# Running the next unit's scores directly behind each unit's values in a fused attention and expert kernel

## The chip, the cores and the metric

The kernel runs on one core of a Trainium2 chip. The metric is the device time of one execution in microseconds (us). Five engines work side by side: PE (TensorE, the matrix array, with its weight loads listed as PEld), DVE (VectorE), ACT (ScalarE), POOL (GpSimd) and SP (SyncE, which issues most transfers). Each runs its own instructions in the order in which the program lists them and waits on semaphores of the others.

## What is computed

Three layers, one behind the other, all in fp32 accuracy:

```python
# 1: attention with a decaying state, B=4 sequences, H=8 heads, 768 steps, D=48
f = 1 / (1 + exp(-f_logit))
for t in range(768):
    state = f[t][:, None] * state + outer(k[t], v[t])
    y[t] = q[t] @ state
# 2: x is y as 3072 rows of 384
h = x @ w_in                      # 384 x 2048
x = (h - tanh(h)) @ w_out         # 2048 x 384
# 3: each row with x @ w_skip > 0 goes to the expert of its largest x @ w_gate
out = x + gate * (relu(x @ w1[e]) @ w2[e])     # 8 experts, 384 x 1024 x 384
```

## The kernel before

**Attention.** The 768 steps of a sequence are cut into 6 chunks of 128; a chunk of one sequence, with all 8 heads, is a unit `u`, and there are 24 of them (`u = 4 * chunk + sequence`). Two units make a block `blk` of 256 rows for layer 2. The steps of a unit, all written in `attend(u)`, are:

- preparation: `lhi`, `llo` (DVE, split the logarithms of f), `pl` (PE, running sums over the chunk, L421), `ek`, `en` (ACT), `mk`, `mq` (DVE, L433 and L436), `tk`, `tq` (PE, transposes, L446) and `ck`, `cq` (ACT, copies out of PSUM);
- `scores` (PE): 32 matmuls q·k (L467) on 48 rows by 64 columns of the array, and from the second chunk on 16 matmuls of q with the old state S (L476), which start the unit's output `py`;
- two `mask` steps (DVE, L496);
- `values` (PE): 16 matmuls of the masked scores with v, added to `py` (L508, 128 rows by 48 columns), and behind them 16 for the change of the state, `pu` (L515, 128 rows by 64 columns);
- `out1`, `out2` (ACT, L537, L538, L541) copy `py` out of PSUM, `renew` (DVE, L559) adds `pu` to S, and `decay` (POOL) multiplies S.

**Layer 2.** Each block has 16 slots. Slot `n` holds `G` (9 matmuls into `ph`, L651) and `H` of the slot two before (6 matmuls into `po`, L691); between them lie `T` and `ghi` on ACT, `bend` on DVE (L663) and `glo` on POOL (L674). Behind a block's last slot its rows are routed (`dot`, L233 on DVE; `pp`, L718 and L719 on PE).

**PSUM.** The pools `pa`, `yp`, `ph` and `po` have two banks each. `scores` takes both banks of `pa` (given back by the masks) and both of `yp` (given back by `out1` and `out2`); `pu`, `pl`, `tk`, `tq` and `pp` take one bank of `pa` each. Block 1 of layer 2 uses `yp` for its sums, so unit 6 can take it only when that block is done.

**The order of the instructions.** For all of attention and the first 10 blocks of layer 2 a planner, `in_order`, sets the order before the program is built. Each step has an engine, a cost in us, the steps that it comes after, the banks that it takes and gives, and a key. The planner repeats: of all steps that can begin, take the one that could begin first, and of equal ones that with the smallest key. The keys are slot numbers; `at(pos)` gives those of attention, 32 slots ahead of the block that needs the unit, the second unit of a block 6 slots behind the first. `T`, `bend`, `ghi` and `glo` have keys 1000 lower than all others. What the planner leaves is one fixed list for each engine. The first 6 units (`FIRST`) run while w_in and w_out are loaded and decoded in 16 chunks (`abs`, `shift`, `stt1`, `stt2`, `hi`, `lo`, mostly on DVE), with keys from -65 up in steps of 6. The last 2 blocks and layer 3 follow in an order written by hand.

Of the kernel before, what the change touches and what calls it, by code (L numbers as in the profile page):

```python
# [9 lines left out]
F32 = mybir.dt.float32  # L10
# [12 lines left out]
LO_BITS = 2.0**-15  # L23
HI_BITS = float.fromhex("0x1.dffffep+16")
MARK = 2.0**-96


class Step:


    def __init__(self, key, eng, cost, emit, after, take, give, moved, lag):
        self.key, self.eng, self.cost, self.emit = key, eng, cost, emit
        self.after, self.take, self.give, self.moved, self.lag = after, take, give, moved, lag
        self.done = None


def in_order(steps, bufs):


    waiting, heirs, ready = {}, {}, []  # L40
    for x in steps:
        waiting[x] = len(x.after)
        for a in x.after:
            heirs.setdefault(a, []).append(x)
        if not x.after:
            ready.append(x)
    taken = {p: [] for p in bufs}
    ended = {}
    free = {}
    left, since, out = {}, 0.0, []  # L50

    def begin(x):
        t = max((a.done + (a.lag if a.eng != x.eng else 0.0) for a in x.after), default=0.0)
        n = {}
        for p, _ in x.take:
            i = len(taken[p]) + n.get(p, 0) - bufs[p]
            n[p] = n.get(p, 0) + 1
            if i >= 0:
                if i >= len(taken[p]) or taken[p][i] not in ended:
                    return None  # L60
                t = max(t, ended[taken[p][i]])
        return max(t, free.get(x.eng, 0.0))

    while ready:
        t, _, _, x = min((t, x.key, i, x) for i, x in enumerate(ready) for t in (begin(x),) if t is not None)
        ready.remove(x)
        free[x.eng] = end = t + x.cost
        if x.moved:
            past = end - since
            while past > 0 and any(left.values()):  # L70
                busy = [e for e in left if left[e]]
                d = min(past / len(busy), min(left[e] for e in busy))
                for e in busy:
                    left[e] = left[e] - d if left[e] - d > 1e-6 else 0.0
                past -= d * len(busy)
            since = max(since, end)
            mine = left[x.eng] = left.get(x.eng, 0.0) + x.moved
            end = since + mine + sum(min(left[e], mine) for e in left if e != x.eng) + 2.0
        x.begun, x.done = t, end
        for p, a in x.take:  # L80
            taken[p].append((p, a))
        for g in x.give:
            ended[g] = end + x.lag
        out.append(x)
        for h in heirs.get(x, ()):
            waiting[h] -= 1
            if not waiting[h]:
                ready.append(h)
    assert len(out) == len(steps), "steps that can never begin"
    return out  # L90
# [3 lines left out]
def decay_attention_moe_kernel(  # L94
# [15 lines left out]
    P = 128  # L110
    B, H, T, D = q.shape
# [15 lines left out]

    AHEAD = 2
    FIRST, NJOIN, NPAY, SKEW = 6, 4, 6, 0
    EARLIEST, LEAD = -100, 32  # L130
    ALONE = 4
    CHUNK0, CHUNK, LATE = -65, 6, 4
    QUEUE = (0, 1, "w", 2, 3, "w", "w", "u", "u", "u", 4, 5, "w", "u")
# [240 lines left out]
        )  # L374
        yield

    xT, xfs, dds = {}, {}, {}

    def side(p, j):

# [4 lines left out]
    def step(name, key, eng, cost, emit, *after, take=(), give=(), moved=0.0, lag=0.15):  # L385

        made[name] = x = Step(key, eng, cost, emit, after, take, give, moved, lag)
        steps.append(x)

    def attend(u):  # L390
# [11 lines left out]
        m = {}  # L402

        def at(pos):
            return (NF * blk - LEAD if u > FIRST - 1 else EARLIEST + 12 * blk) + 6 * half + pos

        def lhi():
            m["hl"] = apool.tile([P, 2, H * D], F32R, tag="lfs", name=f"lfs{u}", bufs=1)
# [49 lines left out]
        def scores():  # L458
            kT, qT = m["kT"], m["qT"]
            ps = m["ps"] = [pa.tile([P, 512], F32, tag="pa", name=f"ps{u}_{j}") for j in range(2)]  # L460
            py = m["py"] = [yp.tile([P, 512], F32, tag="yp", name=f"py{u}_{j}") for j in range(2)]

            def score(p):
                for a in range(2):
                    for j in range(2):
                        r = slice(64 * j, 64 * j + D)
                        nc.tensor.matmul(  # L467
                            ps[j][64 * a : 64 * a + 64, p * P : (p + 1) * P], lhsT=kT[r, p, 64 * a : 64 * a + 64],
                            rhs=qT[r, p], start=True, stop=True,
                        )  # L470

            def recall(p):
                for j in range(2):
                    r = slice(64 * j, 64 * j + D)
                    o, w = 64 * side(p, j), (64, D)[side(p, j)]
                    nc.tensor.matmul(  # L476
                        py[j][o : o + w, p % 2 * P : p % 2 * P + P], lhsT=S[b][r, p, :w], rhs=qT[r, p],
                        start=(p % 2 == 0), stop=False,
                    )

            for p in range(2):
                score(p)
                if c:
                    recall(p)
                    recall(p + 2)
                else:
                    nc.tensor.matmul(
                        py[p][:64, : 2 * P], lhsT=S[b][:, 0].bitcast(BF16)[:, :64],
                        rhs=ones[:112, None, :].to_broadcast([112, 2, P]), start=True, stop=False,
                    )  # L490
                score(p + 2)
# [11 lines left out]
        def values():  # L503
            vt, py = loaded["v", u], m["py"]
            for p in range(NP):
                for j in range(2):
                    o = 64 * side(p, j)
                    nc.tensor.matmul(  # L508
                        py[j][o : o + D, p % 2 * P : p % 2 * P + P], lhsT=vt[:, 2 * p + j], rhs=m["A", j][:, p],
                        start=(c == 0 and o > 0 and p % 2 == 0), stop=(p % 2 == 1),  # L510
                    )
            pu = m["pu"] = pa.tile([P, 512], F32, tag="pa", name=f"pu{u}")
            for h in range(H):
                p, j = divmod(h, 2)
                nc.tensor.matmul(  # L515
                    pu[64 * j : 64 * j + 64, p * D : (p + 1) * D], lhsT=kp[:, h], rhs=vt[:, h], start=True, stop=True
                )
            if u < FIRST:
                for h in range(H):
                    p, j = divmod(h, 2)  # L520
                    nc.tensor.matmul(
                        pu[64 * j : 64 * j + 64, 2 * P + p : 2 * P + p + 1], lhsT=e8[:, h], rhs=ident[:, P - 1 :],
                        start=True, stop=True,
                    )
# [72 lines left out]
        if u >= FIRST:  # L597
# [3 lines left out]
        step(("tq", u), at(1.5), "PE", 0.44, turn4("q", qp4), ("mq", u), ("tk", u), take=((pk_in, f"q{u}"),), lag=0.25)  # L601
        step(("cq", u), at(1.5), "ACT", 0.59, copy4("q"), ("tq", u), ("scores", u - 2), give=((pk_in, f"q{u}"),))
        step(
            ("scores", u), at(2), "PE", 1.5 if c else 1.0, scores, ("ck", u), ("cq", u), ("decay", u - B), ("values", u - 1), 
            take=[("pa", f"s{u}{j}") for j in range(2)] + [("yp", f"y{u}{j}") for j in range(2)], lag=0.25,
        )
        for j in range(2):
            step(
                ("mask", u, j), at(2.5), "DVE", 0.68, mask(j), ("scores", u), ("values", u - 2),
                ("mask", u, j - 1) if j else None, give=(("pa", f"s{u}{j}"),),  # L610
            )
        step(("values", u), at(3), "PE", 1.7 if u < FIRST else 1.3, values, ("mask", u, 1), ("v", u), take=(("pa", f"u{u}"),), lag=0.25)
        step(
            ("out1", u), at(3.5), "ACT", 0.6, out1, ("values", u), ("xlo", u - 1 - half) if blk > 1 else None, ("out2", u - 1),
            give=(("yp", f"y{u}1"),),
        )
        step(("out2", u), at(3.5), "ACT", 0.38, out2, ("out1", u), give=(("yp", f"y{u}0"),))
        old = [("decay", 2 * blk - 4), ("decay", 2 * blk - 3), ("in_range", 2 * blk - 3)]
        step(
            ("renew", u), at(3.5), "DVE", 0.5 if u < FIRST else 0.36, renew, ("values", u),  # L620
            *(old if u < FIRST and half == 0 else []), give=(("pa", f"u{u}"),),
        )
        if u < FIRST:
# [116 lines left out]
        yield  # L740

    def route(u):
        pt = pay.pop(u)
        lg = rpool.tile([P, E + 1], F32, tag="lg", name=f"lg{u}")
        yield from dots(rpool, pt[:, :DM], f"{u}", wb, lg)
        yield from place(pt, lg, u)

    def route_now(u):

        pt = pay.pop(u)  # L750
        px = pa.tile([P, 512], F32, tag="pa", name=f"px{u}")[:, :DM].rearrange("p (k t) -> p k t", k=KT)
        for i in range(KT):
            nc.tensor.transpose(px[:, i], pt[:, i * P : (i + 1) * P], ident)
# [242 lines left out]

    for u in range(NU):
        blk, half = divmod(u, 2)
        e = EARLIEST + 6 * u if u < FIRST else NF * blk - LEAD + 6 * half - 8

        def get(nm, u=u):
            return lambda: load_in(nm, u)
# [29 lines left out]
    for n, (b, f) in enumerate(slots):  # L1032
# [12 lines left out]
        if n < len(slots) - LAG:  # L1045
# [6 lines left out]
            if f == NF - 1:  # L1052
                for u in (2 * b, 2 * b + 1):
                    step(
                        ("fin", u), n + LAG, "ACT", 0.5, (lambda u=u: finish1(u)), ("H", n), ("scat", u - NPAY),
                        ("wb", 0), ("fill", 0) if u == NPAY - 1 else None, give=((p, f"o{b}{u % 2}"),),
                    )
                    step(("out", u), n + LAG + 1, "SP", 0.45, (lambda u=u: finish2(u)), ("fin", u), moved=1.1)
# [431 lines left out]
```

## Time and profile before

| | |
|---|---|
| three timed runs | 734.79, 735.40, 737.32 us, median 735.4 us |
| the profiled execution | 737.04 us, of which the profile's span is 734.9 us |
| mean granted clock of TensorE | 0.988 of full speed |
| PE busy | 696.7 us, 95% of the span |
| DVE, ACT, POOL busy | 67%, 50%, 39% of the span |

The span runs from the first to the last instruction. A busy share is a mean over stages; starts of instructions are measured, ends of matmuls are modelled, so costs on PE are best read from one start to the next.

### The profile page before, as it was taken

Reading aid. Unit: us, or ns where it says so; the run is one execution under the profiler, and the core shown is the slowest. Engines: PE = TensorE matmul, PEld = TensorE weight load, DVE = VectorE, ACT = ScalarE, POOL = GpSimd, SP = SyncE. Lnnn points to the kernel's source line nnn. Section 1 sums busy time; section 2 is a strip of 40 time slices with the busy share of each in tenths; the row PEclk is TensorE's granted clock in tenths of the full one; section 3 lists DMA queues with packets and bytes.
Section 4 is the critical chain, followed back from the end, with each engine's and each line's share of the span. In section 5 each row is a group of like instructions: output and inputs, shape, how many; then the busy total and the mean of one; then the engine's idle time right before and its main releaser. Section 6 shows DMA issues by size and latency. Waiting matters only on the chain. (4 is left out here: it accounts for less than half of the span.)

```text
span 734.9 us, 16491 instructions
## 1 busy us (share of the span) xinstructions
PE 696.7 (95%) x6168; PEld 655.8 (89%) x6168; DVE 491.9 (67%) x1390; ACT 367.0 (50%) x882; POOL 283.2 (39%) x316
## 2 busy tenths in 40 slices
PE   5889989999999999999999999999989899999993
PEld 3678989999998999999999999999989689999993
DVE  2678999678777968768685775845583845655530
ACT  3576786446444465456545444444434435555530
POOL 1232443423344343442434343434543314555641
PEclk9999999999999999999999999999999999999997
DMA  9979793833321312222221220033002667666500
GB/s 155 234 136 220 160 158 80 310 64 72 76 39 40 80 37 70 44 61 44 63 61 28 60 42 32 2 97 115 13 28 71 205 202 236 213 207 211 175 14 22
DMA packets 152688, 76.77 MB, mean 104 GB/s; under 512 B 113864, under 2 KB 149337, under 8 KB 152470
## 3 DMA queue, kind: packets, MB, share of 16 engines
q1 hardware_dynamic: 149462, 70.48, 38.6%
q0 software_dynamic: 2848, 5.00, 1.9%
q8 instruction: 50, 0.82, 0.5%
q14 instruction: 40, 0.33, 0.2%
q10 hardware_dynamic: 288, 0.15, 0.1%
HBM read 61.60 MB, written 15.86 MB: 105 GB/s over the span
## 5 line engine op out<-in xcount | busy, mean ns | idle before, releaser
L674 POOL TENSOR_TENSOR gs<-th,gs 128x256 fp32r<-128x256 f32 x190 | 168.1, 889 | 249.5 <-ACT gs L668 225.0
L691 PE MATMUL po<-uhi,gs 128*128 128x384 f32 x768 | 230.6, 343 | 2.0 <-POOL gs L674 1.8
L651 PE MATMUL ph<-xT,whi 128*128 128x256 f32 x1152 | 219.9, 287 | 2.7 <-DVE th L663 1.8
L651 PEld LDWEIGHTS ph<-xT,whi 128*128 128x128 f32 x1152 | 183.9, 189 | 8.0 <-DVE th L663 3.6
L651 PE MATMUL ph<-xT,wlo 128*128 128x256 f32 x576 | 162.6, 282 | 0.0
L691 PEld LDWEIGHTS po<-uhi,gs 128*128 128x128 f32 x768 | 142.4, 190 | 6.4 <-POOL gs L674 3.8
L663 DVE TENSOR_TENSOR th<-ph,th 128x256 f32<-128x256 f32 x192 | 79.9, 419 | 90.8 <-ACT th L658 90.1
L233 DVE CUSTOM_DVE_ANT_0 scr<-pay,wb 128x384 f32<-128x384 f32 x198 | 128.0, 647 | 7.9 <-ACT pay L699 4.1
L691 PE MATMUL po<-ulo,gs 128*128 128x384 f32 x384 | 129.8, 338 | 0.4 <-DVE ulo L372 0.4
L658 ACT ACTIVATE th<-ph 128x256 f32<-128x256 f32 x192 | 72.7, 381 | 113.2 <-PE ph L651 75.9
L668 ACT ACTIVATE gs<-th 128x256 fp32r<-128x256 f32 x192 | 79.2, 416 | 96.4 <-DVE th L663 92.7
L651 PEld LDWEIGHTS ph<-xT,wlo 128*128 128x128 f32 x576 | 109.5, 190 | 0.0
L691 PEld LDWEIGHTS po<-ulo,gs 128*128 128x128 f32 x384 | 73.2, 191 | 0.7 <-DVE ulo L372 0.7
L1150 PE MATMUL eh<-xt,w 128*128 128x256 f32 x504 | 69.6, 283 | 0.0
L1174 PE MATMUL eo<-w,h 128*128 128x384 f32 x336 | 69.1, 342 | 0.0
L1150 PEld LDWEIGHTS eh<-xt,w 128*128 128x128 f32 x504 | 67.0, 188 | 0.4
L1174 PEld LDWEIGHTS eo<-w,h 128*128 128x128 f32 x336 | 56.3, 188 | 0.0
L1159 DVE SCALAR_TENSOR_TENSOR h<-eh,h 128x256 fp32r<-128x256 f32 x56 | 23.7, 423 | 45.5 <-ACT h L1158 45.5
L1158 ACT ACTIVATE h<-eh 128x256 fp32r<-128x256 f32 x56 | 21.5, 385 | 61.9 <-PE eh L1150 61.8
L732 POOL DMA_INDIRECT xs<-pay,di x24 | 25.7, 1069 | 65.5 <-DVE sm L245 31.2
L317 POOL TENSOR_TENSOR w<-r,w 128x768 fp32r<-128x768 f32 x24 | 44.1, 1846 | 12.3 <-ACT w L316 12.2
L891 POOL DMA_INDIRECT out_dram<-yo,xa x16 | 15.7, 979 | 69.3 <-DVE yo L899 33.6
(189 smaller groups left out, 927.8 us busy)
## 6 DMA issues: line engine op xcount, KB each, us to landing
r<-in_moe_w_dram SPq DMA_DIRECT2D x56, 384.0 KB, 5.1
stgu<-in_moe_w_out_dram SPq DMA_DIRECT2D x4, 1536.0 KB, 7.0
f<-in_f_logit_dram SPq DMA_DIRECT2D x24, 192.0 KB, 3.5
stgw<-in_moe_w_in_dram SPq DMA_DIRECT2D x24, 192.0 KB, 5.5
out_dram<-pay SPq DMA_DIRECT2D x24, 192.0 KB, 2.9
k<-in_k_dram SPq DMA_DIRECT2D x22, 192.0 KB, 3.3
q<-in_q_dram SPq DMA_DIRECT2D x22, 192.0 KB, 3.3
v<-in_v_dram SPq DMA_DIRECT2D x22, 192.0 KB, 2.8
```

The lines of the kernel that those rows point to most:

```text
L233: nc.vector.tensor_tensor_reduce(out=scr, in0=x, in1=wb[:, n], scale=1.0, scalar=0.0, op0=ALU.mult, op1=ALU.add, accum_out=lg[:, n : n + 1])
L317: eng.tensor_tensor(lo, raw, hi.bitcast(F32), ALU.subtract)
L651: nc.tensor.matmul(ph, lhsT=w[:, i, fs], rhs=x[:, i, a], start=(n == 0), stop=(n == 3 * KT - 1))
L658: nc.scalar.activation(th, ph, AF.Tanh)
L663: nc.vector.tensor_tensor(th, ph, th, ALU.subtract)
L668: nc.scalar.activation(t[:, 0], th, AF.Copy)
L674: eng.tensor_tensor(t[:, 1], th, t[:, 0].bitcast(F32), ALU.subtract)
L691: nc.tensor.matmul(po[blk, s], lhsT=t[:, a, ss], rhs=w[:, f], start=(f == 0 and n == 0), stop=(f == NF - 1 and n == 2))
L732: nc.gpsimd.indirect_dma_start(xs[:, :], bass.IndirectOffsetOnAxis(ap=di[:, :], axis=0), pt[:, :], None, bounds_check=E * NT - 1, oob_is_e ...
L1150: nc.tensor.matmul(ph, lhsT=a1[:, w, i, f * P : (f + 1) * P], rhs=xt[:, i, a], start=(n == 0), stop=(n == 3 * KT - 1))
L1159: nc.vector.scalar_tensor_tensor(out=h[:, 1], in0=ph, scalar=0.0, in1=h[:, 0].bitcast(F32), op0=ALU.max, op1=ALU.subtract)
L1174: nc.tensor.matmul(eo[e, s], lhsT=h[:, a, ss], rhs=a2[:, w, f], start=(f == 0 and n == 0), stop=(f == NF2 - 1 and n == 2))
```

## The change

For units from 6 on, `values` is cut in two: `pu` (the 16 matmuls for the state) comes first, at the key that `values` had, and the 16 matmuls into `py` follow as `values`. `renew` now waits for `pu` alone. `values`, and the `scores` of the unit after it, get the key -2000, and the planner counts them as if they could begin 0.5 us earlier (`NEXT`), so that PE goes on with `pu`, `values`, and the next unit's `scores`. So that this unit is ready by then, the steps of preparation get keys 12 lower (`PREP`), as do the loads and the logarithms that feed them, and all of attention 4 lower (`LEAD` 36 in place of 32). The two outputs `py` of successive units lie in the left and right halves of the same two banks of `yp`, which are taken once at unit 6 and not given back; `scores` of a unit comes after `out2` of the unit two before. In the planner each change of PE between these three kinds of step and all others costs 0.2 us (`CHANGE`). The rest keeps `pay` tiles in their table and has `fin` come after the write of the rows that used the same buffer.

```diff
+CHANGE, NEXT = 0.2, 0.5
...
     while ready:
-        t, _, _, x = min((t, x.key, i, x) for i, x in enumerate(ready) for t in (begin(x),) if t is not None)
+        t, _, _, x = min((t - x.ahead, x.key, i, x) for i, x in enumerate(ready) for t in (begin(x),) if t is not None)
+        t += x.ahead
         ready.remove(x)
+        if x.eng == "PE" and x.parts != parts:
+            t, parts = t + CHANGE, x.parts
...
-    EARLIEST, LEAD = -100, 32
+    EARLIEST, LEAD, PREP = -100, 36, 12
...
+        x.parts = name[0] in ("scores", "pu", "values")
+        x.ahead = NEXT if key == -2000 else 0.0
...
-            return (NF * blk - LEAD if u > FIRST - 1 else EARLIEST + 12 * blk) + 6 * half + pos
+            return (NF * blk - LEAD - (PREP if pos < 2 else 0) if u > FIRST - 1 else EARLIEST + 12 * blk) + 6 * half + pos
...
-            py = m["py"] = [yp.tile([P, 512], F32, tag="yp", name=f"py{u}_{j}") for j in range(2)]
+            if u <= FIRST:
+                halves[:] = [yp.tile([P, 512], F32, tag="yp", name=f"py{u}_{j}") for j in range(2)]
+            o = 2 * P * (u % 2) if u >= FIRST else 0
+            py = m["py"] = [t[:, o : o + 2 * P] for t in halves]
...
+            if u < FIRST:
+                update()
+
+        def update():
+            vt = loaded["v", u]
             pu = m["pu"] = pa.tile([P, 512], F32, tag="pa", name=f"pu{u}")
...
         step(
-            ("scores", u), at(2), "PE", 1.5 if c else 1.0, scores, ("ck", u), ("cq", u), ("decay", u - B), ("values", u - 1), 
-            take=[("pa", f"s{u}{j}") for j in range(2)] + [("yp", f"y{u}{j}") for j in range(2)], lag=0.25,
+            ("scores", u), -2000 if u > FIRST else at(2), "PE", 1.5 if c else 1.0, scores, ("ck", u), ("cq", u), ("decay", u - B), ("values", u - 1),
+            ("out2", u - 2), take=[("pa", f"s{u}{j}") for j in range(2)] + ([("yp", f"y{u}{j}") for j in range(2)] if u <= FIRST else []), lag=0.25,
         )
...
-        step(("values", u), at(3), "PE", 1.7 if u < FIRST else 1.3, values, ("mask", u, 1), ("v", u), take=(("pa", f"u{u}"),), lag=0.25)
+        if u >= FIRST:
+            step(("pu", u), at(3), "PE", 0.4, update, ("mask", u, 1), ("v", u), take=(("pa", f"u{u}"),), lag=0.25)
+            step(("values", u), -2000, "PE", 0.9, values, ("pu", u), lag=0.25)
+        else:
+            step(("values", u), at(3), "PE", 1.7, values, ("mask", u, 1), ("v", u), take=(("pa", f"u{u}"),), lag=0.25)
...
-        e = EARLIEST + 6 * u if u < FIRST else NF * blk - LEAD + 6 * half - 8
+        e = EARLIEST + 6 * u if u < FIRST else NF * blk - LEAD - PREP + 6 * half - 8
...
-                        ("fin", u), n + LAG, "ACT", 0.5, (lambda u=u: finish1(u)), ("H", n), ("scat", u - NPAY),
+                        ("fin", u), n + LAG, "ACT", 0.5, (lambda u=u: finish1(u)), ("H", n), ("scat", u - NPAY), ("out", u - NPAY),
```

## Rows read from the trace of the kernel before

**Rows 1.** The page's busy time, share of the span and instructions, for PE.

```profile
PE 696.7 (95%) x6168; PEld 655.8 (89%) x6168; DVE 491.9 (67%) x1390; ACT 367.0 (50%) x882; POOL 283.2 (39%) x316
```

**Rows 2.** Windows: length, then busy us and instructions by engine, clock, transfers.

```profile
100.00:120.00 20.00, 18.53 (x126) 17.29 (x125) 19.90 (x27) 14.61 (x33) 8.37 (x9) 1.00 0.76 150
...
140.00:490.00 350.00, 347.31 (x3495) 330.46 (x3495) 260.46 (x850) 175.64 (x460) 134.43 (x159) 1.00 0.24 55
```

**Rows 3.** Waits of PE from 140 to 500 us: total, times, longest.

```profile
PE po L691 <- POOL gs L674: 1.5, 2, 0.9
...
PE py L508 <- DVE A L496: 0.3, 2, 0.2
```

**Rows 4.** Timeline of PE around one unit's scores: start, duration, what.

```profile
328.13 0.34 PE L691 MATMUL po<-uhi,gs 128*128 128x384 f32 x1
328.40 0.45 PE L467 MATMUL ps<-qT,kT 48*64 48x128 f32 x8
328.67 0.40 PE L476 MATMUL py<-qT,S 48*64 48x128 f32 x8
328.89 0.62 PE L467 MATMUL ps<-qT,kT 48*64 48x128 f32 x16
329.32 0.40 PE L476 MATMUL py<-qT,S 48*64 48x128 f32 x8
...
329.87 0.44 PE L691 MATMUL po<-uhi,gs 128*128 128x384 f32 x1
```

**Rows 5.** Timeline of PE around the same unit's values.

```profile
332.19 1.08 PE L508 MATMUL py<-A,v 128*48 128x128 f32 x16
333.11 0.62 PE L515 MATMUL pu<-v,kp 128*64 128x48 f32 x16
333.66 0.44 PE L691 MATMUL po<-uhi,gs 128*128 128x384 f32 x1
333.94 0.34 PE L691 MATMUL po<-ulo,gs 128*128 128x384 f32 x1
334.11 0.51 PE L691 MATMUL po<-uhi,gs 128*128 128x384 f32 x2
```

**Rows 6.** Timeline of the weight loads behind those values.

```profile
333.00 0.60 PEld L515 LDWEIGHTS pu<-v,kp 128*64 128x64 f32 x16
333.65 0.19 PEld L691 LDWEIGHTS po<-uhi,gs 128*128 128x128 f32 x1
```

**Rows 7.** Weight loads of an early unit, from a half-wide tile to transposes.

```profile
31.02 0.55 PEld L521 LDWEIGHTS pu<-ident,en 128*64 128x64 f32 x16
31.59 0.41 PEld L446 LDWEIGHTS pk<-ident,early 128*112 128x112 f32 x4
```

**Rows 8.** Timelines of PE and DVE: `pu` and `renew`, the latest of 18 and a usual one.

```profile
305.50 0.62 PE L515 MATMUL pu<-v,kp 128*64 128x48 f32 x16
...
306.81 0.35 DVE L559 TENSOR_TENSOR S<-pu,S 112x192 f32<-112x192 f32 x1
...
333.77 0.36 DVE L559 TENSOR_TENSOR S<-pu,S 112x192 f32<-112x192 f32 x1
```

**Rows 9.** Timeline of ACT: `out1` (first copy) and `out2`.

```profile
333.56 0.26 ACT L537 ACTIVATE tm<-py 112x128 f32<-112x128 f32 x1
...
333.87 0.39 ACT L541 ACTIVATE xf<-py 112x256 f32<-112x256 f32 x1
```

**Rows 10.** Timeline of the loading stage, DVE and PE: preparation of units 6 and 7.

```profile
92.44 0.35 DVE L409 CAST lfs<-f 128x384 fp32r<-128x384 f32 x1
92.83 0.56 DVE L412 TENSOR_TENSOR lfs<-f,lfs 128x384 fp32r<-128x384 f32 x1
...
120.81 0.55 DVE L433 TENSOR_TENSOR kp<-k,kp 128x384 f32<-128x384 f32 x1
121.27 1.10 DVE L436 TENSOR_TENSOR qp<-q,en 128x384 f32<-128x384 f32 x1
...
92.85 0.44 PE L421 MATMUL pl<-lfs,tri 128*128 128x384 f32 x1 [1.72 <-DVE lfs L409]
```

More of the change, by code (lines that the diff above doesn't have):

```diff
@@ L34, in __init__ @@
         self.done = None
+        self.parts, self.ahead = False, 0.0
 def in_order(steps, bufs):
@@ L50, in in_order @@
     left, since, out = {}, 0.0, []
+    parts = False
     def begin(x):
@@ L375, in unpack @@
         yield
-    xT, xfs, dds = {}, {}, {}
+    xT, xfs, dds, halves = {}, {}, {}, []
     def side(p, j):
@@ L611, in attend @@
             )
-        step(("values", u), at(3), "PE", 1.7 if u < FIRST else 1.3, values, ("mask", u, 1), ("v", u), take=(("pa", f"u{u}"),), lag=0.25)
+        if u >= FIRST:
[3 more added lines that the diff above has]
+            step(("values", u), at(3), "PE", 1.7, values, ("mask", u, 1), ("v", u), take=(("pa", f"u{u}"),), lag=0.25)
         step(
             ("out1", u), at(3.5), "ACT", 0.6, out1, ("values", u), ("xlo", u - 1 - half) if blk > 1 else None, ("out2", u - 1),
-            give=(("yp", f"y{u}1"),),
+            give=(("yp", f"y{u}1"),) if u < FIRST else (),
         )
-        step(("out2", u), at(3.5), "ACT", 0.38, out2, ("out1", u), give=(("yp", f"y{u}0"),))
+        step(("out2", u), at(3.5), "ACT", 0.38, out2, ("out1", u), give=(("yp", f"y{u}0"),) if u < FIRST else ())
         old = [("decay", 2 * blk - 4), ("decay", 2 * blk - 3), ("in_range", 2 * blk - 3)]
         step(
-            ("renew", u), at(3.5), "DVE", 0.5 if u < FIRST else 0.36, renew, ("values", u),
+            ("renew", u), at(3.5), "DVE", 0.5 if u < FIRST else 0.36, renew, ("values" if u < FIRST else "pu", u),
             *(old if u < FIRST and half == 0 else []), give=(("pa", f"u{u}"),),
@@ L742, in route @@
     def route(u):
-        pt = pay.pop(u)
+        pt = pay[u]
         lg = rpool.tile([P, E + 1], F32, tag="lg", name=f"lg{u}")
@@ L748, in route_now @@
     def route_now(u):
-        pt = pay.pop(u)
+        pt = pay[u]
         px = pa.tile([P, 512], F32, tag="pa", name=f"px{u}")[:, :DM].rearrange("p (k t) -> p k t", k=KT)
```

## The prediction

> **What bounds the kernel now.** I read the page first, then windows, waits and the timeline of single units. PE is busy for 95% of the span, no other engine for more than 67% [rows 1]. In the stage where units 6 to 23 run, from 140 to 490 us, PE is busy 347.3 of 350 us at full granted clock while DVE has 90 us and ACT 174 us to spare [rows 2]. The idle 2.7 us there go mostly to late `gs` tiles, which the change does not touch, and 0.3 us to masks that `values` waited for [rows 3]. So time can be won in this stage only by giving PE less to do. The number of matmuls stays the same; what may shrink is what PE loses where small tiles of the array follow whole ones. The start, by contrast, is bound by DVE: from 100 to 120 us it is busy 19.90 of 20 us and PE idles 1.47 us [rows 2].
>
> **The change part by part, first the price of a switch.** Ends of matmuls are modelled, so I count from start to start. Within `H` one matmul follows another after 334.11 - 333.94 = 0.17 us [rows 5].
>
> Going into `scores`: the last matmul of `H` starts at 328.13, so the next could start at 328.30; it starts at 328.40, 0.10 us later. The first 8 take 0.27 us, where 16 in the middle take 0.43, so 0.215 for 8: 0.05 us more [rows 4]. Sum 0.15.
>
> Coming back from `pu`: its 16 weight loads begin at 333.00 and end at 333.60, the next load begins at 333.65: 0.05 us. Then the first matmul of `H` needs 333.94 - 333.66 = 0.28 us in place of 0.17, since its weights could not be loaded ahead: 0.11 us [rows 5, 6]. Sum 0.16.
>
> From `values` to `pu`, both on tiles of 128 rows by half the columns, 16 matmuls take 333.11 - 332.19 = 0.92 us [rows 5], that is 57 ns each for 128 columns, and I see no step at the joint. Turning the two round costs and saves nothing.
>
> **What the joint removes and adds.** For units 7 to 23, 17 times, one return (0.16) and one entry (0.15) vanish: 0.31 us. In their place stands one step from `values` (128 rows) to `scores` (tiles of 64 rows) that the trace does not show at full speed. It costs from nothing, as between `values` and `pu`, to 0.31 us, if the narrower row tiles need both the emptying and the late weights. The one half-wide tile followed directly by another form without PE waiting lost 31.59 - 31.57 = 0.02 us [rows 7], but that went to whole tiles. The nearest row is the entry into `scores` itself, from 128 rows to 64: 0.15 us. I take it. Gain 0.16 us a joint, 17 x 0.16 = 2.7 us, bounds 0 and 5.3.
>
> The planner's own count makes the step from `values` to `scores` free; that alone would give 5.3 us. A rule speaks against it. The Trainium skill (TensorEngine Tiling (Array Packing), Key Properties) says that a change of the tiling mode, not of the tile alone, drains the array, and it lists 128x64 and 64x64 as different modes; by it three of the four drains of a unit would stay. The rows agree so far: a gap into `scores` [rows 4], none within one mode [rows 5]. The sum by the rule is the one I took.
>
> **What the joint may wait for.** `scores` needs both banks of `pa`, one held by `pu` until `renew` has read it. From the start of `pu` to the end of `renew` passes 334.13 - 333.11 = 1.02 us as usual, and 307.16 - 305.50 = 1.66 us at worst [rows 5, 8]. With `pu` first and `values` behind it PE is busy for 0.55 + 0.92 = 1.47 us, and the step takes 0.15. So `values` hides `renew`; without this cover every joint would pay 0.4 us. The worst case leaves 0.05 to 0.2 us once: 0.1 us lost. The planner may let PE idle up to 0.5 us for `scores`; that is a rival below.
>
> **The halves of a bank.** If the reading of one half and the writing of the other are kept apart, `out1` of a unit, issued behind the next `scores`, waits until these are done, 1.5 us later. Queued behind it on ACT are `out2`, copies of the preparation, and later `T` and `ghi`. During the chain of 0.55 + 0.92 + 1.5 = 3 us PE finishes no `G`, so the `T` and `ghi` of the last one run before `out1`, and the next `T` is due only after it; ACT has half its time free [rows 2]. I cost it at nothing; without the cover it would be up to 1 us each time.
>
> **Masks, preparation, loads.** `pu` now comes well after its masks, not 2 to 4 us behind `scores`: the 0.3 us of waits [rows 3] go. Preparation 12 slots earlier changes no work; `pl` of a unit still waits for `values` of the unit two before, so in the steady stage it lies in PE's stream as now. The earlier loads (f, k, q, v on SP's queue) still wait for the same weight load and pass only later entries. In the start it is a rival. `CHANGE` makes the plan's 2.8 us for a pair of `scores` and `values` 3.2, near the real 1.47 + 1.47 + entries and returns: fewer small waits at best, which I do not price. The edits to `pay` and `fin` cost nothing: the write of a row block is long done when its buffer comes round.
>
> **The sum.** -2.7 - 0.3 + 0.1 = -2.9 us. The profiled run took 737.0 us with a span of 734.9; the same shape would give a span of 732.0 and a run of 734.1. That execution is at the top of the three runs; from their median of 735.4 the sum gives 732.5 us.
>
> **Rivals.**
> 1. *The joint is free* (one mode, as the planner counts). For: [rows 7]. Against: the entry into `scores` [rows 4]. 17 x 0.31 = 5.3, with the other terms -5.5: 729.9 us.
> 2. *The change doesn't show*: the step from `values` to `scores` costs as much as the two that it replaces, or the plan finds preparation or `renew` late and puts a `G` between, so that few joints exist. For: `renew`'s margin is thin in the plan (0.25 + 0.36 + 0.15 against 0.9 us), and DVE is 74% busy [rows 2]. Gain 0 to 1: about 735 us.
> 3. *The start gets slower.* Keys of preparation for units 6 and 7 fall from 16 and 22 to 0 and 6, ahead of the last chunks of the weights (keys 1 to 25), and the `CHANGE` cost shifts the plan of units 0 to 5. One unit's `lhi`, `llo`, `mk`, `mq` are 0.35 + 0.56 + 0.55 + 1.10 = 2.6 us on the engine that bounds this stage [rows 10]; two units 5.1 us, if PE waits for all of it. `pl` has already cost PE 1.72 us there. Against: `lhi` of unit 6 ran at 92.4 us, ahead of chunks with smaller keys, so time and not key decided. At the full price: 732.5 + 5.1 = 737.6 us. It decides once over 2.9 us are lost before 140 us. The other unit's preparation can't move there, since `pl` of unit 8 waits for `values` of unit 6.
> 4. *A bank as a lock on PE.* If the plan puts `out1` and `out2` ahead of the next `scores`, its 16 matmuls into the other half wait for the copies, which end 334.26 - 333.56 = 0.7 us after they begin [rows 9], some 1.0 us after `values`, less 0.2 us of q·k work first: 17 x 0.8 = 14 us, 746 us. Against: `scores` may go 0.5 us ahead and `out1` is planned 0.25 us behind `values`. The Trainium skill (PSUM — Partial Sum Buffer, PSUM bank collisions raise a hardware error) holds that TensorE and ScalarE must not touch one bank and quadrant at once, whatever the columns; no row here shows two units in one bank.
>
> **How the numbers follow.** Forecast 0.43, at 732.5 us, its own range 730.5 to 734 (waits and the step's cost by a third either way); rival 1 0.13; rival 2 0.20; rival 3 0.16; rival 4 0.04; 0.04 for a gain beyond rival 1 from a tighter plan. A measurement tells 0.3%, 2.2 us, from no change: faster is below 733.2, slower above 737.6. Two thirds of the forecast's 0.43 lie below 733.2 (0.29), and with rival 1 and the last case 0.46, to which rival 2's better plans add 0.04: faster 0.50. Rival 3 gives 0.10 slower and 0.06 same, rival 4 0.04 slower, and 0.02 of rival 2 falls there with a worse plan: slower 0.16. The rest is the same, 0.34. The range leaves out rival 4, half of rival 1 and of the gains beyond it, and the upper end of rival 3: 729.5 to 737.5.
>
> **What would show it.** In the timeline: `pu`, `values`, `scores` in one block for units 6 to 23, 17 joints. From the last matmul of `values` to the first of `scores` a gap near 0.10 us and no idle time released by `renew`. `out1` starting about 1.5 us later behind `values`. PE's idle time in the stage near 2.4 us. The length of the stretch from unit 6's scores to unit 23's values, for the same slots, 3 us shorter, and the start up to there unchanged within 1 us. Wrong if `renew` releases PE at joints, if `G` or `H` lie between `values` and the next `scores`, if the start moves by more than 2 us, or if `gs` tiles come later because ACT is held up.

## The result

| | before | after |
|---|---|---|
| median of four runs each | 736.36 us (734.79 to 738.49) | 746.30 us (744.79 to 749.23) |
| ratio after / before, 95% interval | | 1.0143 (1.0113 to 1.0173) |
| profiled execution, its span | 737.04, 734.9 us | 749.23, 747.3 us |
| mean granted clock | 0.988 | 0.979 |

The change costs 9.9 us. The forecast was 732.5 us with a range up to 737.5: wrong in sign, and outside.

From the page of the kernel after, busy time by engine and the clock in 40 slices:

```profile
PE 705.4 (94%) x6168; PEld 659.1 (88%) x6168; DVE 483.5 (65%) x1390; ACT 366.0 (49%) x882; POOL 286.5 (38%) x316
...
PEclk9978999999999999999999999999999999999997
```

The clock on the page of the kernel before:

```profile
PEclk9999999999999999999999999999999999999997
```

The same 6168 matmuls keep PE busy 8.7 us longer than in [rows 1], and the third and fourth slices, 37 to 75 us, show a lower clock than before. So the loss isn't only idle time, and a part of it lies where no joint is yet. (Line numbers differ between kernels: in the kernel after, `G` is L672, `H` L712, `scores` L479 and L488, `values` L520, `pu` L532 and `renew` L576.)

To place it I read three points in each timeline: the start of unit 6's scores (called S6), a matmul near the end of the planned part (P: 559.3 us before, 572.0 after) and the end. S6 is 141.45 us before and 150.27 after, with the same number of `G` and `H` ahead of it: **8.8 us lost in the start**. From S6 to P, 417.85 us became 421.7: **3.9 us lost in the steady stage**, where a gain was forecast. From P to the end 175.6 became 175.3. (The sum is that of two single executions, 12.2 us apart; the one after was the slowest of its four.)

**The start.** Windows of the kernel after, and the same of the kernel before behind it; columns as in [rows 2]:

```profile
40.00:60.00 20.00, 18.27 (x180) 15.49 (x177) 13.51 (x25) 13.49 (x32) 7.33 (x7) 0.74 0.71 116
60.00:80.00 20.00, 16.69 (x207) 15.02 (x206) 14.42 (x23) 11.99 (x29) 4.92 (x7) 0.83 0.79 185
```

```profile
40.00:60.00 20.00, 16.82 (x163) 13.29 (x167) 17.41 (x29) 16.18 (x38) 7.10 (x9) 0.94 0.77 155
60.00:80.00 20.00, 20.00 (x284) 19.14 (x277) 16.64 (x28) 11.49 (x28) 7.68 (x8) 0.97 0.84 177
```

From 40 to 60 us PE is busier after than before and DVE has 3.9 us less work: the matmuls are slow (clock 0.74), and what DVE needs from them seems to come late; that this is why DVE has less to do is read from the order, and no run tests it alone. From 60 to 80 us PE makes 207 matmuls instead of 284. The timeline of PE after, from this stretch:

```profile
42.35 0.49 PE L827 MATMUL pg<-ident,wg 128*9 128x128 f32 x3 [1.20 <-DMA wg<-in_moe_w_skip_dram]
...
49.34 0.63 PE L672 MATMUL ph<-xT,whi 128*128 128x256 f32 x2
49.77 0.41 PE L672 MATMUL ph<-xT,wlo 128*128 128x256 f32 x1
49.98 0.63 PE L672 MATMUL ph<-xT,whi 128*128 128x256 f32 x2
...
53.78 1.08 PE L520 MATMUL py<-A,early 128*48 128x128 f32 x16
...
66.86 0.38 PE L672 MATMUL ph<-xT,whi 128*128 128x256 f32 x1 [2.70 <-ACT xT L597]
```

And two lines of that of the kernel before, the values of the same unit 3 and S6:

```profile
45.37 1.08 PE L508 MATMUL py<-A,early 128*48 128x128 f32 x16
...
141.45 0.45 PE L467 MATMUL ps<-qT,kT 48*64 48x128 f32 x8
```

The transposes of the gate's weights (`pg`) now stand ahead of the first `G`, where their transfer hasn't landed. PE then runs at half the clock: three matmuls of `G` take 49.98 - 49.34 = 0.64 us, against 0.36 us at full clock, up to 53 us. Unit 3's values start at 53.78 us, 8.4 us later than before, and PE later waits 2.7 us for the rows of a block that these values lead to.

**The joint.** Timeline of PE after, around the block of [rows 4, 5]:

```profile
330.25 0.67 PE L532 MATMUL pu<-v,kp 128*64 128x48 f32 x16
330.75 1.05 PE L520 MATMUL py<-A,v 128*48 128x128 f32 x16
331.73 0.45 PE L479 MATMUL ps<-qT,kT 48*64 48x128 f32 x8
332.00 0.40 PE L488 MATMUL py<-qT,S 48*64 48x128 f32 x8
...
332.87 0.40 PE L479 MATMUL ps<-qT,kT 48*64 48x128 f32 x8
333.20 0.50 PE L672 MATMUL ph<-xT,whi 128*128 128x256 f32 x2
```

It is as drawn: one block without idle time. `values` takes 331.73 - 330.75 = 0.98 us up to `scores`; 16 such matmuls take 0.91, so the step costs 0.07 us, and the first 8 of `scores` again 0.27, 0.05 more than in the middle. But there are 13 such joints, not 17: ahead of the scores of units 8, 9, 10 and 18 the plan put other work.

**What waits.** Waits of PE after, from 140 to 520 us (columns as in [rows 3]), and two lines of all engines' from 150:

```profile
PE po L712 <- POOL gs L695: 2.2, 5, 0.7
PE ps L479 <- DVE S L576: 1.9, 3, 0.9
...
ACT th L679 <- PE ph L672: 40.0, 55, 2.5
ACT tm L554 <- PE py L488: 22.0, 13, 2.5
```

`renew` releases PE three times, which before it never did, and late `gs` cost 2.2 instead of 1.5 us [rows 3]. The last line is new: ACT stands idle 22 us until the scores' last matmul into `py` (L488) is done, before it may copy the other half of that bank. Summed from one start to the next (stretches on PE more than 0.25 us over their matmuls' usual time, called stalls below), the stalls from S6 to P went from 8.9 to 11.9 us. The level depends on how the usual time is taken: a recount of every matmul, from its start to the next start, less the median for the same tiles, gives 6.1 and 10.8 us, and for the other kernels up to 2.7 us less than the table below. Differences of stalls under 2 us say little.

### The profile page after: what moved, and what is told of

It reads as the page before. It is cut to its first block, busy times and chain, and to the rows that moved or that the text cites. A ratio compares the mean times of both kernels' runs of the same rounds, so it can differ in the third digit from the quotient of the medians.

```text
span 747.3 us, 16492 instructions
## 1 busy us (share of the span) xinstructions
PE 705.4 (94%) x6168; PEld 659.1 (88%) x6168; DVE 483.5 (65%) x1390; ACT 366.0 (49%) x882; POOL 286.5 (38%) x316
## 5 line engine op out<-in xcount | busy, mean ns | idle before, releaser
L695 POOL TENSOR_TENSOR gs<-th,gs 128x256 fp32r<-128x256 f32 x190 | 170.9, 902 | 249.0 <-ACT gs L689 239.5
L712 PE MATMUL po<-uhi,gs 128*128 128x384 f32 x768 | 230.4, 343 | 3.6 <-POOL gs L695 3.2
L672 PE MATMUL ph<-xT,whi 128*128 128x256 f32 x1152 | 223.4, 290 | 6.4 <-ACT xT L597 2.7
L672 PEld LDWEIGHTS ph<-xT,whi 128*128 128x128 f32 x1152 | 186.8, 192 | 13.5 <-issue 4.6
L672 PE MATMUL ph<-xT,wlo 128*128 128x256 f32 x576 | 164.1, 285 | 0.0
L712 PEld LDWEIGHTS po<-uhi,gs 128*128 128x128 f32 x768 | 141.0, 189 | 10.2 <-POOL gs L695 8.6
L684 DVE TENSOR_TENSOR th<-ph,th 128x256 f32<-128x256 f32 x192 | 79.9, 418 | 82.5 <-ACT th L679 81.6
L712 PE MATMUL po<-ulo,gs 128*128 128x384 f32 x384 | 129.3, 337 | 0.0
L689 ACT ACTIVATE gs<-th 128x256 fp32r<-128x256 f32 x192 | 79.5, 416 | 95.7 <-DVE th L684 91.4
L672 PEld LDWEIGHTS ph<-xT,wlo 128*128 128x128 f32 x576 | 111.1, 193 | 0.0
L712 PEld LDWEIGHTS po<-ulo,gs 128*128 128x128 f32 x384 | 73.0, 190 | 0.1
L508 DVE TENSOR_TENSOR A<-ps,tri 128x512 f32<-128x512 f32 x48 | 31.2, 682 | 20.2 <-PE ps L479 20.2
```

The lines of the kernel that those rows point to most:

```text
L508: nc.vector.tensor_tensor(m["A", j], m["ps"][j].rearrange("s (p t) -> s p t", p=NP), tri[:, None, :].bitcast(F32).to_broadcast([P, NP, P]) ...
L672: nc.tensor.matmul(ph, lhsT=w[:, i, fs], rhs=x[:, i, a], start=(n == 0), stop=(n == 3 * KT - 1))
L684: nc.vector.tensor_tensor(th, ph, th, ALU.subtract)
L689: nc.scalar.activation(t[:, 0], th, AF.Copy)
L695: eng.tensor_tensor(t[:, 1], th, t[:, 0].bitcast(F32), ALU.subtract)
L712: nc.tensor.matmul(po[blk, s], lhsT=t[:, a, ss], rhs=w[:, f], start=(f == 0 and n == 0), stop=(f == NF - 1 and n == 2))
```

## The experiments

"Count" is the planner's `CHANGE`. S6 is corrected for one `G` and `H` more or less ahead of it (2.1 us the pair), S6 to P by the same. The run of before beside each kernel had a median of 736.3 to 736.5 us, in the last batch (e13 to e15) 735.1. So kernels of different batches are compared by the ratio too, which sets each against the runs of before in its own batch.

| kernel | median (range), us | ratio (95%) | S6 | S6 to P | stalls | joints |
|---|---|---|---|---|---|---|
| before, profile | | | 141.5 | 417.9 | 8.9 | 0 |
| after, profile | | | 150.3 | 421.7 | 11.9 | 13 |
| e1_count_only | 746.1 (744.1 to 747.3) | 1.0127 (1.0104 to 1.0151) | 152.0 | 418.5 | 6.6 | 0 |
| e2_count_late | 743.9 (741.6 to 745.5) | 1.0108 (1.0076 to 1.0140) | 141.9 | 423.4 | 15.7 | 13 |
| e3_prep_only | 737.3 (734.5 to 738.7) | 1.0005 (0.9983 to 1.0027) | 142.0 | 417.0 | 7.4 | 0 |
| e4_no_count | 737.9 (732.9 to 743.6) | 1.0022 (0.9990 to 1.0053) | 142.7 | 417.9 | 7.7 | 13 |
| e5_renew_first | 738.0 (734.4 to 742.8) | 1.0015 (0.9992 to 1.0039) | 147.2 | 417.8 | 9.3 | 15 |
| e6_renew_out | 733.5 (731.2 to 739.0) | 0.9963 (0.9938 to 0.9987) | 143.6 | 413.6 | 7.5 | 14 |
| e7_dve_costs | 740.7 (739.3 to 743.3) | 1.0056 (1.0039 to 1.0074) | 147.4 | 419.3 | 12.6 | 12 |
| e8_all | 732.3 (729.8 to 733.8) | 0.9933 (0.9907 to 0.9958) | 142.3 | 413.0 | 6.8 | 14 |
| e9_early_count | 741.6 (738.0 to 743.1) | 1.0070 (1.0045 to 1.0095) | 147.4 | 414.2 | 8.4 | 13 |
| e10_gate_late | 738.9 (734.0 to 740.2) | 1.0018 (0.9998 to 1.0038) | 150.8 | 411.6 | 6.8 | 14 |
| e11_costs_no_joint | 741.7 (739.0 to 745.3) | 1.0063 (1.0041 to 1.0086) | 142.3 | 420.6 | 11.6 | 0 |
| e12_all_no_count | 733.8 (730.3 to 736.6) | 0.9952 (0.9932 to 0.9972) | 145.0 | 411.9 | 7.6 | 14 |
| e13_count_from_4 | 736.2 (733.8 to 740.1) | 1.0025 (1.0002 to 1.0048) | 147.2 | 411.8 | | 14 |
| e14_count_not_4_5 | 739.3 (737.3 to 740.9) | 1.0063 (1.0038 to 1.0087) | 148.0 | 414.2 | | 13 |
| e15_gate_first | 734.9 (731.1 to 737.3) | 0.9998 (0.9981 to 1.0016) | 144.8 | 411.6 | | 14 |

S6, S6 to P and stalls are of one execution each. S6 isn't fixed by the order alone: e4, e5 and e6 have the same order up to there, and 142.7, 147.2 and 143.6 us. So for the start the medians and ratios decide.

**e1_count_only**: the kernel before with the count alone.

```diff
+        if x.eng == "PE" and x.parts != parts:
+            t, parts = t + CHANGE, x.parts
...
+        x.parts = name[0] in ("scores", "pu", "values")
```

> The kernel before, with only the planner's 0.2 us for each change between scores, values and other steps on PE; nothing of attention is joined. Theory A (the count, applied to units 0 to 5 as well, reorders the start): the start of unit 6's scores moves from 141.5 us to about 150 us as in the changed kernel, and the time rises by 7 to 11 us. Theory B (the earlier keys of preparation and loads make the start late): the start stays within 1.5 us of before and the time within 0.5%. Theory C (joint and waits in the steady stage carry the loss): no change at all here.

The count alone costs 1.27% and puts S6 10.5 us later. Waits of its PE from 36 to 145 us:

```profile
PE pg L812 <- DMA wg<-in_moe_w_skip_dram: 4.7, 1, 4.7
PE ph L657 <- ACT xT L586: 2.5, 1, 2.5
```

Theory A comes out. These are the two waits of the kernel after; the first is longer here, 4.7 us against 1.2, for the transposes begin only at 45.02 us, and after at 42.35.

**e2_count_late**: the kernel after, the count only for units from 6 on.

```diff
-        x.parts = name[0] in ("scores", "pu", "values")
+        x.parts = name[0] in ("scores", "pu", "values") and name[1] >= FIRST
```

> The changed kernel, with the 0.2 us counted only for units from 6 on. Theory A: the first 60 us keep the order of before, unit 6's scores start at 141 to 144 us, and the time falls by 7 to 9 us, to about 738 us. Theory B: unit 6's scores stay near 150 us and the time near 746. In the steady stage some 4 us more than before remain either way, if late renew steps and late gs tiles are what the joint brought.

S6 comes back to 141.9 us, as theory A had it; but the time falls by 2.4 us and not by 7 to 9, which isn't clear of noise (1.0108 against 1.0143, the intervals overlap). The steady stage gets longer, 423.4 us against 421.7. Waits of all its engines from 150 to 520 us, PE's lines:

```profile
PE po L712 <- POOL gs L695: 2.3, 6, 0.6
PE ps L479 <- DVE S L576: 2.0, 3, 1.1
...
PE pk L455 <- DVE kp L442: 1.4, 3, 0.9
PE pp L739 <- DVE A L508: 1.3, 2, 0.8
```

**e3_prep_only**: the kernel before with the new keys of preparation.

```diff
-    EARLIEST, LEAD = -100, 32
+    EARLIEST, LEAD, PREP = -100, 36, 12
```

> The kernel before, with only the earlier keys: LEAD 36, PREP 12 for preparation and loads. Theory B: unit 6's scores start 5 us or more later and the time rises by 5 us or more. Theory A: unit 6's scores start within 2 us of 141.5 us, time within 0.5% of before.

No difference clear of noise: in the kernel before, rival 3's reason, preparation ahead of the last weights, is out.

**e4_no_count**: the kernel after without the count.

```diff
-CHANGE, NEXT = 0.2, 0.5
+CHANGE, NEXT = 0.0, 0.5
```

> The changed kernel with the count set to 0 and all else kept: joints, halves, earlier preparation. Theory A: the start as before, time 736 to 740. If the plan's truer count for the steady stage is worth something, this is 1 to 2 us slower than the kernel that counts from unit 6 on; if not, equal within 0.3%.

8.4 us of the median come back, and joints without the count still bring no gain over before. 13 joints' worth is lost elsewhere. This kernel is also 6.0 us faster than e2: with these joints the count from unit 6 on doesn't help the plan of the steady stage, it makes it worse.

**e5_renew_first** (theory D: `renew` is late because of its key) and **e6_renew_out** (theory E: planning `out1` where the bank lets it run). e5 is e4 with the first line, e6 has both; in both the head start `NEXT` stays with PE's steps, so that `renew` gets the key alone:

```diff
-            ("renew", u), at(3.5), "DVE", ...
+            ("renew", u), at(3.5) if u < FIRST else -2000, "DVE", ...
...
-            ("out1", u), at(3.5), "ACT", 0.6, out1, ("values", u), ...
+            ("out1", u), at(3.5), "ACT", 0.6, out1, ("values", u), ("scores", u + 1) if FIRST <= u < NU - 1 else None, ...
```

> The changed kernel with the count at 0 and renew of units from 6 on given the key -2000, so that the plan sets it ahead of dots and bends on DVE. Theory D (scores wait for the bank that renew gives back late): PE's waits for renew fall from 1.6 us below 0.5 us and the stage from unit 6's scores on gets 1 to 2 us shorter than without this key; time about 736 us. Rival: the waits only go to another step of DVE, time 737 to 738 as before.

> As the run with renew first, and the plan sets out1 behind the next unit's scores, where the shared bank holds it anyway. Theory E (out1 held by the bank holds ghi behind it on ACT, so gs tiles come late): PE's waits for gs tiles fall from 1.9 us below 0.5 us, the idle time of ACT ahead of out1 falls from 26 us below 8 us, and the time is 1 to 2 us lower than with renew first alone. Rival (ACT has time enough): ACT's idle time moves, the waits for gs and the time stay.

e5 gains nothing, and `renew` still holds PE, by stalls 1.9 us: theory D falls. e6 is 4.5 us faster than e5 and 0.37% faster than before. Waits of e5, then of e6, from 150 to 520 us:

```profile
ACT tm L554 <- PE py L488: 22.5, 13, 2.5
...
PE ps L479 <- DVE S L576: 1.2, 2, 1.0
PE po L712 <- POOL gs L695: 1.2, 4, 0.4
```

```profile
ACT tm L554 <- PE py L488: 13.4, 10, 2.5
...
PE ps L479 <- DVE S L576: 0.8, 2, 0.6
...
PE po L712 <- POOL gs L695: 0.7, 2, 0.4
```

The gain is shown, theory E's path to it only in part. ACT's idle time ahead of `out1` falls by 9.1 us, to 13.4 and not below 8; late `gs` fall by 0.5 us, to 0.7 and not below 0.5; and the time falls by more than the 1 to 2 us that E gave. The stage is 4.2 us shorter, the stalls only 1.8 us. In the recount of all starts the other 2.4 us lie in delays of less than 0.25 us each, 1.2 of them between the matmuls of `H`, which read `gs`.

**e7_dve_costs** (theory F: the count is right, and hurts since DVE's costs are too low): e2 with costs as the traces have them.

```diff
-            step(("llo", u), at(0), "DVE", 0.47, ...
+            step(("llo", u), at(0), "DVE", 0.74, ...
-        step(("mk", u), at(1), "DVE", 0.56, ...
+        step(("mk", u), at(1), "DVE", 0.56 if u < FIRST else 0.79, ...
-                            ("dot", u, i), at + 0.6 * i, "DVE", 0.64, ...
+                            ("dot", u, i), at + 0.6 * i, "DVE", 0.73, ...
```

(`mq` as `mk`; `lhi` 0.36 to 0.41.) **e8_all**: e7 with the two edits of e5 and e6.

> The kernel with the count from unit 6 on, and with the planner's DVE costs of preparation and dots at the means of the trace (0.41, 0.74, 0.79, 0.79, 0.73 in place of 0.36, 0.47, 0.56, 0.56, 0.64 us). Theory F (counting PE's changes alone makes the plan believe that DVE is earlier than it is, hence 16 us of stalls on PE against 8 without the count): stalls fall to 8 to 10 us, time from 744 to about 738 us. Rival G (the longer plan itself, with joints at other places, costs the time): stalls stay above 13 us, time 742 or more.

> All together: count from unit 6 on, renew first, out1 behind the next scores in the plan, DVE costs from the trace. If D, E and F hold: stalls below 7 us, 14 joints, time 733 to 735 us, the first to beat the kernel before. If the count is harmful whatever the other costs: 740 or more.

e7 wins 3.2 us over e2, half of what F asked; its stalls of 12.6 us lie between F's 8 to 10 and G's 13. e8 is the fastest version: 0.9933, 4.1 us under before. Its interval overlaps that of e6 (0.9963), which has neither the count nor the truer costs, so what these two add isn't shown. Its page and its waits from 150 to 520 us:

```profile
PE 690.3 (95%) x6168; PEld 651.7 (89%) x6168; DVE 486.2 (67%) x1390; ACT 368.3 (51%) x882; POOL 287.5 (39%) x316
```

```profile
ACT tm L554 <- PE py L488: 13.2, 10, 2.5
...
PE ps L479 <- DVE S L576: 0.2, 1, 0.2
```

PE is busy 6.4 us less than before [rows 1], `renew` hardly holds it, and `gs` no longer does.

**e11_costs_no_joint** (theory J: the joints are worth having; K: the right costs alone do it): the kernel before with e7's costs and e2's count. **e12_all_no_count**: e8 with `CHANGE` 0.

> The kernel before without joints or halves, with the truer DVE costs and the count from unit 6 on. Theory J (the joint itself is worth 14 x 0.17 = 2.4 us once its waits are gone): this stays within 0.4% of before, 734 to 739 us, so 2 us or more above the fastest. Rival K (the fastest kernel wins by the truer plan, not by the joint): 731 to 733 us.

> The fastest kernel with the count at 0. If a true count helps once the other steps are planned truly: 1 to 3 us slower, 733.5 to 735.5 us. If the count has no value: equal within 1 us.

Without joints the same planner makes 741.7 us, slower than before: K is refuted. J's number isn't met either, for it allowed 0.4% over before, and e11 is 0.63% over. From S6 to P e11 takes 7.5 us more than e8, of which 14 joints explain 2.4; its stalls are 4.8 us higher. So the truer costs helped one kernel (e7 against e2) and with the count harmed the other. In e8 the count of the steady stage makes 1.5 us (732.3 against 733.8), not clear of noise.

**What in the early count costs so much?** **e9_early_count** is e8 with the count for all units again; **e10_gate_late** is e9 with the gate's transposes behind the third `G`; **e15_gate_first** is e8 with the first `G` behind these transposes; **e13_count_from_4** and **e14_count_not_4_5** count some early units.

```diff
-        x.parts = name[0] in ("scores", "pu", "values") and name[1] >= FIRST
+        x.parts = name[0] in ("scores", "pu", "values")
...
-    step(("turn", 0), -1000, "PE", 0.4, ..., ("scores", 2), ("preset", 0), ...
+    step(("turn", 0), -1000, "PE", 0.4, ..., ("scores", 2), ("preset", 0), ("G", 2), ...
```

> The fastest kernel so far (renew first, out1 behind the next scores, DVE costs from the trace), with the count of 0.2 us applied to units 0 to 5 as well. Theory A: only the start changes; unit 6's scores begin 7 to 10 us later and the time rises from 732 to 739 to 742 us. Rival: the start's delay in the changed kernel came from something else or is taken back later, time within 2 us of 732.

> As the kernel with the early count, but the three transposes of the gate weights must come after the third G, so that PE cannot wait for their transfer ahead of the first G. Theory H (the count costs the start because it puts these transposes ahead of G 0 and values of unit 3 behind G 2, with PE idle and the clock at half behind it): most of the delay goes, unit 6's scores within 3 us of 142, time 733 to 736 us. Rival: the order of the later steps (transposes and G of block 1) costs it, time stays above 738 us.

> The fastest kernel with the count from unit 4 on (two early units more). The order up to the transposes of unit 5 is that of the fastest kernel. Theory L (the start is lost where units 0 to 3 are counted, since there the gate's transposes and the values of unit 3 change places): 732 to 734 us, unit 6's scores near 142 to 144 us. Rival M (any counted early unit costs its share): 735 to 738 us.

> The fastest kernel with the count for units 0 to 3 and from 6 on. Theory L: the whole price of the early count, 739 to 742 us, with waits for the gate weights and for xT of block 1. Rival M: 736 to 739 us.

> The fastest kernel, without early count, but the first G must come after the gate's transposes. Theory N (PE standing in front of the gate weights' transfer with the first G behind it is what costs the start): 735 to 740 us. Rival (the late values of unit 3 and with them xT of block 1 are what costs; here these values come early): 732 to 734 us.

e9 against e8: 9.4 us by the medians, 10.1 by the ratios, for six early units' count, in a kernel that is otherwise the best: theory A holds. (e9's profile is of its fastest execution, 738.0 us, so its S6 is on the early side.) With the gate's transposes behind the third `G` (e10) their wait is gone and 2.7 us come back by the medians, 3.8 by the ratios; but the time stays above 738 us and S6 at 150.8, as H's rival said. So this wait is a part, and not most of it.

e15 doesn't test that wait, though it was made for it. The plan set unit 3's scores ahead of the transposes, and when these could start it was a mask that released them:

```profile
44.16 0.50 PE L827 MATMUL pg<-ident,wg 128*9 128x128 f32 x3 [0.80 <-DVE A L508]
```

e15 is slower than e8 all the same, by 2.7 us (medians) or 4.8 (ratios), and theory N stays open.

Counting units 4 and 5 alone (e13) costs 3.9 us by the medians and 6.8 by the ratios, units 0 to 3 alone (e14) 7.0 and 9.6; a difference of two ratios is good to some 2.5 us. Theory L, which gave units 4 and 5 nothing, falls; units 0 to 3 alone cost nearly the whole, and the parts need not add up.

## Why the prediction was wrong

**The step that failed** is the one on the count: "fewer small waits at best, which I do not price", and with it "the start up to there unchanged within 1 us". The count applies to units 0 to 5 too, and by e1, alone, it costs 9.8 us of the median: it changes which steps the planner thinks can begin, in the stage where loads, decoding and PE are all close to the limit. Some 3 to 4 us go with the gate's transposes ahead of their transfer (e10 against e9). Late values, the wait for `xT` and stretches at half clock go with the rest, and which of these is cause and which is effect stays open. The half clock is not needed for a late start: e13 has S6 4.9 us later than e8 at the same granted clock, 1.00 from 40 to 80 us in both (of such a gap 2.7 us can be chance, for e12 has e8's order up to S6 and 145.0 us). Nor is the start all that the count costs: confined to units from 6 on it leaves 6.0 us more than no count (e2 against e4), so it harms the plan of the steady stage as well, and the two costs don't add up. Rival 3 named the place and the count, but priced another mechanism, which e3 shows to cost nothing.

**The step from `values` to `scores`** was right: 0.07 us ahead of `scores` and 0.05 over its first 8 matmuls, in sum 0.12 for 0.15 forecast. A pair took 0.095 + 0.91 + 0.55 + 0.10 + 0.095 + 1.47 + 0.10 = 3.32 us (entry, values, `pu` with the gap behind it, late weights of `H`, entry, scores, return) and takes 0.095 + 0.50 + 0.98 + 1.47 + 0.10 = 3.145: 0.175 us a joint, 0.16 forecast. The Trainium skill (TensorEngine Tiling (Array Packing), Key Properties) says that a change of mode drains the array; the 0.07 us agree. Rival 1's free joint is out by them. The number of joints was taken as 17 and is 13: 2.3 us, not 2.7.

**`renew`** was costed at 0.1 us, "So `values` hides `renew`"; by stalls it measured 3.0, in three joints. The cover of 1.47 us was right; the late end wasn't bounded by [rows 8], since in the new order `dot`s or other steps of DVE lie ahead of `renew`. PE, then DVE, at the first of the three (the longest wait, at unit 14's scores, was 0.94 us):

```profile
198.25 0.67 PE L532 MATMUL pu<-v,kp 128*64 128x48 f32 x16
...
199.73 0.43 PE L479 MATMUL ps<-qT,kT 48*64 48x128 f32 x2
200.87 0.33 PE L479 MATMUL ps<-qT,kT 48*64 48x128 f32 x3 [0.71 <-DVE S L576]
```

```profile
199.40 0.54 DVE L240 CUSTOM_DVE_ANT_0 scr<-pay,wb 128x384 f32<-128x384 f32 x1
...
199.98 0.56 DVE L240 CUSTOM_DVE_ANT_0 scr<-pay,wb 128x384 f32<-128x384 f32 x1
...
200.46 0.35 DVE L576 TENSOR_TENSOR S<-pu,S 112x192 f32<-112x192 f32 x1
```

`renew` ends 2.56 us after `pu` began. Its key alone doesn't mend that (e5, 1.2 us of waits); with all edits together 0.2 us are left (e8).

**The halves of a bank**: "I cost it at nothing" was the other wrong zero. The mechanism was right: `out1` comes 1.64 us late. But its cover wasn't there. ACT after, behind the joint shown above, then a line of DVE and one of PE:

```profile
333.12 0.28 ACT L554 ACTIVATE tm<-py 112x128 f32<-112x128 f32 x1 [1.64 <-PE py L488]
333.30 0.27 ACT L555 ACTIVATE xf<-py 112x128 f32<-112x128 f32 x1
333.45 0.39 ACT L558 ACTIVATE xf<-py 112x256 f32<-112x256 f32 x1
333.72 0.73 ACT L689 ACTIVATE gs<-th 128x256 fp32r<-128x256 f32 x2
```

```profile
332.30 0.74 DVE L684 TENSOR_TENSOR th<-ph,th 128x256 f32<-128x256 f32 x2
```

```profile
335.44 0.34 PE L712 MATMUL po<-uhi,gs 128*128 128x384 f32 x1
```

Two `ghi` (L689) are queued behind the held copies: both `bend`s (L684) are done at 333.04 us, and the first `ghi` begins at 333.72. Here PE loses nothing by it, for `H` follows at 335.44 without idle time; over the stage PE's waits for `gs` are 0.7 us longer than before. With the copy planned where the bank lets it run, the kernel is 4.5 us faster (e6 against e5), more than these waits account for. Rival 4 put the lock on PE, at 746 us; that its number is near the result is chance, for PE shows no wait on the copies. The Trainium skill (PSUM — Partial Sum Buffer, PSUM bank collisions raise a hardware error) asks that two engines be kept apart by bank and quadrant, or more simply by bank, and not by address. The program does so by bank, and here 22 us of ACT's idle time are its price.

**Masks**: the forecast of 0.3 us less wasn't tested by itself. **In sum**: the median lost 9.9 us, and by e4 8.4 us of that hang on the count. From S6 to P the two profiles differ by 3.9 us; stalls give 3.0 (4.7 in the recount) and the joints -2.3, so some 1.5 to 3 us there aren't placed. The premise that time can be won there only by giving PE less to do was too narrow: e8 is 4.8 us shorter from S6 to P than before, and its 14 joints are 2.4 of that.

## What to carry to other kernels

A cost in a static planner is not a local edit: one number meant for one stage reorders every stage in which that engine takes part, so before pricing such a change, list where else it applies, and test it alone (e1). To confine it (e2) brought the start back, and of the time hardly anything. Waits that an edit adds to an engine with idle time are not free because the engine has time: to give the planner the dependence was worth 4.5 us here (e6 against e5). Costs set right in part made this kernel slower than before (e2, e7, e11); with that dependence in the plan it was faster, with the truer costs (e8) or without them (e6).

## What the runs showed of the hardware that was not expected

At the same order of instructions the start took 142.7, 147.2 and 143.6 us (e4, e5, e6), with granted clocks of 1.00, 0.83 and 0.93 in the window from 60 to 80 us. In the kernel after, PE waited for the gate's weights and then ran at 1.2 GHz for some 10 us while it had work nearly throughout; from the mean of 0.74 in 40 to 60 us, 0.26 x 20 / 0.5 = 10.4 us were at the lower level, so that 5.2 us more work would have fitted at the full one. But idle time alone doesn't tell it: e8 idled 3.3 us in that window, more than the kernel after, at a clock of 1.00. The window of e8:

```profile
40.00:60.00 20.00, 16.69 (x187) 13.34 (x191) 17.30 (x29) 16.50 (x39) 7.10 (x9) 1.00 0.76 154
```
